# First attention of a four-layer kernel: row transposes in another order, q weights in two loads, mask copies later, one v product earlier

## The chip, the cores and the metric

The kernel runs on one core of one Trainium2 chip. Times are device microseconds (us) of one execution. A kernel is described by the median of its runs, with the lowest and the highest. Engines are named as the profile does: PE is TensorE, PEld its weight loads, DVE VectorE, ACT ScalarE, POOL GpSimd, SP SyncE, which here only issues DMAs. A "q" behind an engine's name marks a DMA issue in its queue.

## The reference

Four layers on x of 2048 x 576, each with a residual: attention A, mixer B, A, B. Only A matters here.

```python
def A(x, wqkv, wo):                      # x: layernormed, 2048 x 576, 32 heads of 18
    q, k, v = split(x @ wqkv)
    idx  = pos[:, None] - 2 * arange(8)  # each query sees 8 keys, every second one back
    attn = softmax(where(idx >= 0, q . k[idx] * 18**-0.5, -1e9))
    return (attn @ v[idx]) @ wo
x = x + A(layernorm(x), A_wqkv, A_wo)
x = x + B(layernorm(x), ...)             # gelu, 2048 x 2048 spatial mix, product
# ... and the same two again
```

## The kernel before

An attention tile is 112 queries; there are 19, each in two half steps, so the main loop runs over steps s = 0 to 37: scores (L_mm) for the next step, exponential (EXP), product with v (PV). Other work is hung on steps by `at(step, function, ...)`: projections PG of q and k, products VW for v, output projection WO, and behind it the layernorm of the next layer's input, LN_XN, with its row transpose LN_T, a DMA issued by SyncE. PG writes q and k into a staging buffer; DMAs then move them into QK, heads spread over the partitions. QK has extra rows for the window's mask, filled by VectorE (`fill_window_rows`).

```python
def fill_window_rows(self, QK, half):
    ...
    for g0 in (0, 4):                    # four copies of 128 x 4096
        for a in range(2):
            nc.vector.tensor_copy(out=QK[:, a, g0:g0 + 4, c0:c0 + n]..., in_=self.pat[...]...)

def load_wqk(self, eng):
    for c0, n, w0 in ((D, 512, D + 64), (0, D, 0), (D + 512, 64, D)):   # k, q, rest of k
        ...
# ---- schedule of an attention layer (li == 0: the first)
for i in range(NS):                      # 16 row blocks of 128
    ...
    at(s, WO, i, 0)                      # needs the row transpose oT<-o_t of its tile
    at(s + 1, WO, i, 1)
    at(s + 2, LN_XN, i)
    if i < NS - 1:
        at(max(s + 4, 24 + (5 * i) // 4) if li == 0 else s + 4, LN_T, i)
if li == 0:
    at(0, self.load_wo, nc.sync)         # 648 KB, needed from step 8
    for f in reversed(self.load_win2a(nc.gpsimd)):
        at(0, f)                         # 6 x 288 KB, needed in the mixer only
...
for k_, (d, qk, cc) in enumerate(pre):   # last projections ahead of the loop
    ...
    PG(d, qk, cc, li > 0 or k_ < 4, q2)
    if li == 0 and k_ == 3:
        self.fill_window_rows(QK, 1)
if li == 0:
    VW(nvw - 1, 0, False)
    VW(nvw - 1, 1, False)
for s in range(NST):
    if s + 1 < NST: L_mm(s + 1); EXP(s + 1)
    PV(s)                                # one more row transpose, oT<-o_t, for SyncE
    for f, a in table.pop(s, []): f(*a)
```

The softmax here doesn't subtract the row's maximum and nothing guards it: scores larger than these inputs give would overflow.

## Time and profile before

| | before |
|---|---|
| first three runs, median (lowest to highest) | 1191.1 us (1190.1 to 1191.19) |
| profiled run: span, granted clock | 1190.8 us, 0.998 |
| TensorE busy | 1180.2 us, 99% |
| first attention | 2 to 134 us |
| all 55 later runs beside the experiments | median 1191.9 us (1189.2 to 1195.4) |

The prediction below shows this kernel's profile line by line. TensorE is busy almost all the time, so a change in DMAs or other engines can win only idle TensorE time, or time in which its clock is halved.

One line that the prediction did not look at is SyncE's queue just before the loop (columns: start, length, engine and line, operation, destination<-source, count):

```profile
41.93 5.20 SPq L249 DMA_TRANSPOSE xnT<-ln_xn  x4
```

The fourth of these is issued by 47.14 us and lands, by its semaphore in the trace, at 50.02 us. The step-1 projection that reads it starts at 50.90 us. There is slack of 0.9 us, and nobody waits in this profile; so the line is easy to pass over.

### The profile page before, as it was taken

To read this page: it belongs to the slowest core of one execution; us is meant where nothing else is said; L and a number is where in the kernel's file an instruction comes from. 1 tells how busy PE (TensorE), PEld (TensorE's weight loads), DVE (VectorE), ACT (ScalarE), POOL (GpSimd) and SP (SyncE) were. 2 spreads that over 40 slices of the span, in tenths; PEclk is the share of its full clock that TensorE was granted. 3 is DMA by queue.
4 is the path that set the end of the run, shared out by engine and by line. 5 is a ranking of instruction groups with operands and counts; after the bars stand their busy time and mean duration, and the time that the engine had idled before them with its cause. 6 is when DMAs were issued, how large, how long until landed. Compare 5 with 4: busy or idle time off the path is not lost.

```text
span 1190.8 us, 20761 instructions
## 1 busy us (share of the span) xinstructions
PE 1180.2 (99%) x8554; PEld 620.6 (52%) x8554; DVE 547.4 (46%) x1206; ACT 376.6 (32%) x593; POOL 281.5 (24%) x383
## 2 busy tenths in 40 slices
PE   8999999999999999999999999999999999999998
PEld 5567544444444444457755775444444444444677
DVE  8688587333233233245556786753233233233311
ACT  5578677210110110202156786760110110111000
POOL 4768685000000000001153877530000000000000
PEclk9999999999999999999999999999999999999999
DMA  8989992000000000049645999900000000000332
GB/s 195 200 163 199 181 224 65 23 4 9 12 12 12 12 1 11 12 139 291 169 98 117 203 227 196 202 14 9 12 12 1 12 12 12 12 1 28 125 105 73
DMA packets 178104, 101.21 MB, mean 85 GB/s; under 512 B 134336, under 2 KB 159360, under 8 KB 178009
## 3 DMA queue, kind: packets, MB, share of 16 engines
q1 hardware_dynamic: 165144, 78.13, 30.6%
q0 software_dynamic: 6512, 16.00, 5.4%
q10 hardware_dynamic: 6352, 5.75, 1.6%
q8 instruction: 67, 1.10, 0.4%
q14 instruction: 29, 0.23, 0.1%
HBM read 42.39 MB, written 16.53 MB: 49 GB/s over the span
## 4 chain that ended last, share of the span: by engine, by line
PE 94%; DMA 3%; POOL 1%; ACT 0%; issue 0%; SPq 0%; DVE 0%; ACTq 0%; DVEq 0%
PE pg L887 42%; PE pz L869 12%; PE po L941 12%; PE pz L791 11%; PE pp L402 5%; PE pw L494 3%; PE O_ps L457 3%; PE pv L379 3%; PE L_ps L437 2%; DMA oT<-o_t 2%; PE pzs L791 1%; DMA QK<-win2a 1%; POOL QK L77 1%; DMA wqk_sb<-in_A_wqkv_dram 1%; ACT P_sb L446 0%
## 5 line engine op out<-in xcount | busy, mean ns | idle before, releaser
L887 PE MATMUL pg<-Wq,Z 128*128 128x512 bf16 x2304 | 502.8, 379 | 0.0
L887 PEld LDWEIGHTS <-Z 128*128 128x128 bf16 x2304 | 225.3, 98 | 272.0
L891 DVE TENSOR_TENSOR g_tmp<-pg,ln_xn 128x512 f32<-128x512 f32 x144 | 99.6, 692 | 429.2 <-PE pg L887 429.2
L881 ACT ACTIVATE z1T<-pz 128x1024 bf16<-128x1024 f32 x72 | 73.7, 1024 | 513.8 <-PE pz L869 513.6
L77 POOL DMA_DIRECT2D wout<-in_B_w_out_dram x4 | 4.3, 1064 | 604.6 <-PE pg L887 604.6
L941 PE MATMUL po<-wout,Z 128*128 128x288 bf16 x1152 | 141.4, 286 | 0.0
L446 ACT ACTIVATE P_sb<-L_ps 128x896 bf16<-128x896 f32 (+1 forms) x152 | 126.7, 887 | 41.2 <-PE L_ps L437 40.6
L869 PE MATMUL pz<-xnT,w 128*128 128x512 bf16 (+1 forms) x640 | 136.0, 380 | 0.0
L941 PEld LDWEIGHTS <-Z 128*128 128x128 bf16 x1152 | 112.7, 98 | 28.8
L791 PEld LDWEIGHTS <-xnT 128*128 128x128 bf16 (+1 forms) x800 | 66.2, 97 | 81.0 <-issue 23.7
L791 PE MATMUL pz<-win2a,xnT 128*128 128x512 bf16 x384 | 104.8, 380 | 0.0
L892 DVE TENSOR_TENSOR Z<-g_tmp,z1T 128x512 bf16<-128x512 f32 x144 | 99.6, 692 | 9.7
L869 PEld LDWEIGHTS <-w 128*128 128x128 bf16 (+1 forms) x640 | 51.1, 97 | 80.0 <-issue 27.1
L402 PE MATMUL pp<-xnT,wqk_sb 128*128 128x512 bf16 x360 | 83.8, 382 | 0.5 <-DMA wqk_sb<-in_A_wqkv_dram 0.5
L805 ACT ACTIVATE zp<-pz 128x1024 bf16<-128x1024 f32 x64 | 65.5, 1024 | 36.6 <-PE pz L791 32.8
L951 DVE TENSOR_TENSOR x_new<-po,xo 128x288 f32<-128x288 f32 (+1 forms) x64 | 28.8, 455 | 87.6 <-PE po L941 83.5
L791 PE MATMUL pz<-win2b,xnT 128*128 128x512 bf16 (+1 forms) x256 | 65.7, 380 | 0.0
L807 DVE CUSTOM_DVE_ANT_0 Z<-zp 128x1536 bf16<-128x1536 bf16 x32 | 56.6, 1769 | 13.1 <-ACT zp L805 13.0
L77 POOL DMA_DIRECT2D QK<-stg x81 | 50.7, 631 | 36.3 <-DVE stg L371 21.0
L379 PE MATMUL pv<-wv_sb,xnT 128*128 128x288 bf16 (+1 forms) x380 | 55.8, 285 | 0.0
L242 POOL TENSOR_SCALAR ln_xn<-x_new,ln_mv,ln_rstd 128x576 bf16<-128x576 f32 x23 | 52.8, 2294 | 2.0
L402 PEld LDWEIGHTS <-wqk_sb 128*128 128x128 bf16 x360 | 33.2, 98 | 37.2 <-DMA wqk_sb<-in_A_wqkv_dram 1.0
(114 smaller groups left out, 916.9 us busy)
## 6 DMA issues: line engine op xcount, KB each, us to landing
xres<-x_new SPq DMA_DIRECT2D x48, 288.0 KB
xo<-xres SPq DMA_DIRECT2D x32, 288.0 KB
wout<-in_B_w_out_dram POOLq DMA_DIRECT2D x4, 1296.0 KB, 8.5
xo<-xres SPq DMA_DIRECT2D x8, 576.0 KB
w<-in_B_w_in_dram SPq DMA_DIRECT2D x16, 256.0 KB
QK<-stg POOLq DMA_DIRECT2D x53, 72.0 KB, 4.4
QK<-stg SPq DMA_DIRECT2D x41, 72.0 KB
xo<-in_A_x_dram SPq DMA_DIRECT2D x8, 288.0 KB
```

The source lines that it names most:

```text
L77: return eng.dma_start(out=out, in_=in_)
L379: nc.tensor.matmul(pv[:nk, 0:288], lhsT=self.xnT[:, c, QT * t:QT * t + nk], rhs=wv_sb[:, c, hh * 288:(hh + 1) * 288], start=(c == 0), stop ...
L402: nc.tensor.matmul(pp[:, :], lhsT=w, rhs=self.xnT[:, c, PADL + cc * 512:PADL + (cc + 1) * 512], start=(c == 0), stop=(c == 4))
L446: nc.scalar.activation(out=P_bufs[(2 * s + jp) % 4][:nk, :, :, 0:nq], in_=Lv[:nk, :, :, 0:nq], func=ACT.Exp, scale=scale)
L791: nc.tensor.matmul(pzvs[ci][:, sub * 512:sub * 512 + w], lhsT=self.xnT[r0:r1, c, PADL + i * P:PADL + (i + 1) * P], rhs=win2(c)[r0:r1, c0 + ...
L805: nc.scalar.activation(out=zp[:, c0:c0 + cn], in_=pzvs[ci][:, 0:cn], func=ACT.Gelu_apprx_tanh, accum_out=sums[:, ci:ci + 1])
L869: nc.tensor.matmul(pz1s[q // 2][:, q % 2, :], lhsT=w1[r0:r1, c, sub * P:(sub + 1) * P], rhs=self.xnT[r0:r1, c, PADL + q * 512:PADL + (q + ...
L881: nc.scalar.activation(out=z1T[:, q2 * 512:(q2 + 2) * 512], in_=pz1s[q2 // 2][:, :, :].rearrange("p a b -> p (a b)"), func=ACT.Gelu_apprx_ ...
L887: nc.tensor.matmul(pg[:, :], lhsT=Z[:, jj, i, sub * P:(sub + 1) * P], rhs=Wq[q][:, i, :], start=(i == 0), stop=(i == NS - 1))
L891: nc.vector.tensor_tensor(out=tmp[:], in0=pg[:, :], in1=bsp[:, qs], op=ALU.add)
L892: nc.vector.tensor_tensor(out=uT(jj)[:, sub, qs], in0=tmp[:], in1=z1Ts[jj, sub][:, qs], op=ALU.mult)
L941: nc.tensor.matmul(acc[hh], lhsT=uT(j // 2)[:, j % 2, i * P:(i + 1) * P], rhs=wouts[j // NJH][:, j % NJH, hh * 288:(hh + 1) * 288], start= ...
```

## The change

The intent: let the first q product start on part of its weights; fill the stop before the first scores with a v product and take the mask copies out of GpSimd's way there; and spread the row transposes so that those of the attention output no longer queue behind them at the end.

```diff
-    def fill_window_rows(self, QK, half):
+    def fill_window_rows(self, QK, half, parts=((0, 0), (0, 1), (4, 0), (4, 1))):
...
-    def load_wqk(self, eng):
+    def load_wqk(self, eng, names=("k", "q", "k1")):
+        parts = dict(k=(D, 512, D + 64), q=(0, D, 0), q0=(0, 256, 0), q1=(256, D - 256, 256), k1=(D + 512, 64, D))
...
-                xn = stgs[(2 + k_) % NSTG]...
+                xn = stgs[(1 + k_) % NSTG]...
...
-            self.load_wqk(nc.sync)
+            self.load_wqk(nc.sync, ("k", "q0", "q1", "k1"))
...
-                VW(t, hh, li == 0)                 # last argument: evict on VectorE
+                VW(t, hh, li == 0 and t > 5)
...
-                    at(13 * hh, VW, t, hh, True)
+                    if hh == 1:
+                        at(0, VW, t, hh, True)
...
-                at(max(s + 4, 24 + (5 * i) // 4) if li == 0 else s + 4, LN_T, i)
+                at(s + 4 if li > 0 or i > 12 else 19 + 2 * i if i < 8 else 35 + (i - 8) // 2, LN_T, i)
         if li == 0:
+            at(1, self.fill_window_rows, QK, 1, ((4, 0),))
+            at(2, self.fill_window_rows, QK, 1, ((4, 1),))
             at(0, self.load_wo, nc.sync)
-            for f in reversed(self.load_win2a(nc.gpsimd)):
-                at(0, f)
+            w2l = self.load_win2a(nc.gpsimd)
+            for k_ in (3, 5, 4, 2, 1, 0):
+                at(0, w2l[k_])
...
-            if li == 0 and k_ == 3:
-                self.fill_window_rows(QK, 1)
...
             VW(nvw - 1, 1, False)
+            VW(nvw, 0, True)
+            self.fill_window_rows(QK, 1, ((0, 0), (0, 1)))
```

More of the change, by code (lines that the diff above doesn't have):

```diff
@@ L193, in fill_window_rows @@
         c0 = PADL + half * n
-        for g0 in (0, 4):
-            for a in range(2):
-                nc.vector.tensor_copy(out=QK[:, a, g0:g0 + 4, c0:c0 + n].rearrange("p g (k x) -> p g k x", x=256),
-                                      in_=self.pat[:, a, None, None, PADL:PADL + 256].to_broadcast([P, 4, n // 256, 256]))
+        for g0, a in parts:
+            nc.vector.tensor_copy(out=QK[:, a, g0:g0 + 4, c0:c0 + n].rearrange("p g (k x) -> p g k x", x=256),
+                                  in_=self.pat[:, a, None, None, PADL:PADL + 256].to_broadcast([P, 4, n // 256, 256]))
     def H_tile(self, name):
@@ L284, in zero_right @@
         nc.vector.memset(R["wo"][64:128, 4, :], 0.0)
-    def load_wqk(self, eng):
+    def load_wqk(self, eng, names=("k", "q", "k1")):
         R = self.right
-        for c0, n, w0 in ((D, 512, D + 64), (0, D, 0), (D + 512, 64, D)):
+        parts = dict(k=(D, 512, D + 64), q=(0, D, 0), q0=(0, 256, 0), q1=(256, D - 256, 256), k1=(D + 512, 64, D))
+        for c0, n, w0 in (parts[k_] for k_ in names):
             self.dma(R["wqk"][:, :, w0:w0 + n], self.A_wqkv[0:512, c0:c0 + n].rearrange("(c p) n -> p c n", p=P), eng=eng)
@@ L509, in LN_XN @@
                 k_, m = divmod(i - 4, 3)
-                xn = stgs[(2 + k_) % NSTG][:].rearrange("p a b -> p (a b)")[:, 640 * m:640 * (m + 1)]
+                xn = stgs[(1 + k_) % NSTG][:].rearrange("p a b -> p (a b)")[:, 640 * m:640 * (m + 1)]
             tails[i]["xn"] = self.ln_xn(tails[i]["x"], P, mv, rstd, nmr, eng="pool", xn=xn)
```

## The prediction

> **What bounds the kernel now.** I read the page first, then the busy times by stretch, then the engines in order of time around the few gaps, then the chain of waits. The page says that TensorE is the bound of the whole program:
>
> ```profile
> span 1190.8 us, 20761 instructions
> ...
> PE 1180.2 (99%) x8554; PEld 620.6 (52%) x8554; DVE 547.4 (46%) x1206; ACT 376.6 (32%) x593; POOL 281.5 (24%) x383
> ```
>
> All that is not TensorE is 1190.8 - 1180.2 = 10.6 us. The change touches the first attention only (about 2 to 134 us); the mixers and the second attention issue the same instructions in the same order. So nearly all of it is settled by idle and slow TensorE time in those 134 us. By stretch (columns: length; PE, PEld, DVE, ACT, POOL busy with counts; granted clock; DMA share; GB/s):
>
> ```profile
> 14.00:24.00 10.00, 9.53 (x49) 4.79 (x50) 8.70 (x29) 5.45 (x10) 1.71 (x2) 1.00 0.79 146
> ...
> 44.00:50.00 6.00, 5.24 (x57) 3.12 (x55) 5.60 (x7) 3.75 (x6) 5.43 (x7) 1.00 1.09 204
> 50.00:54.00 4.00, 4.00 (x68) 1.95 (x67) 2.14 (x5) 1.98 (x4) 1.05 (x2) 0.57 1.07 364
> ...
> 80.00:92.00 12.00, 11.47 (x237) 8.36 (x234) 10.33 (x33) 10.50 (x13) 11.23 (x14) 1.00 0.83 186
> 92.00:102.00 10.00, 9.57 (x198) 7.17 (x197) 7.25 (x23) 9.37 (x14) 9.50 (x10) 1.00 1.11 205
> ...
> 120.00:134.00 14.00, 12.18 (x208) 8.16 (x206) 10.65 (x33) 6.79 (x14) 10.21 (x11) 1.00 1.05 187
> ```
>
> TensorE lacks 0.47 us near 14 us, 0.76 at 44 to 50, 0.53 and 0.43 between 80 and 102, and 1.82 in the last 14 us; and from 50 to 54 us it is busy but at a granted clock of 0.57. That is the whole pool, about 5.3 us when the clock dip counts for 1.2. TensorE in order of time names the releasers:
>
> ```profile
> 14.47 1.90 PE L402 MATMUL pp<-xnT,wqk_sb 128*128 128x512 bf16 x8 [0.55 <-DMA wqk_sb<-in_A_wqkv_dram]
> ...
> 48.86 0.22 PE L437 MATMUL L_ps<-QK 32*128 32x112 bf16 x1 [0.69 <-DMA QK<-win2a]
> ...
> 50.90 2.29 PE L402 MATMUL pp<-xnT,wqk_sb 128*128 128x512 bf16 x5
> ...
> 125.22 0.79 PE L494 MATMUL pw<-wo_sb,oT 128*128 128x288 bf16 x5 [0.59 <-DMA oT<-o_t]
> ...
> 131.51 1.39 PE L494 MATMUL pw<-wo_sb,oT 128*128 128x288 bf16 x10 [1.23 <-DMA oT<-o_t]
> ```
>
> The group at 50.90 took 2.29 us; the same five matmuls take 1.24 us at 54.08 and later. The late waits are on the row transposes of the attention output. SyncE's queue shows why they are late:
>
> ```profile
> 121.02 1.78 SPq L469 DMA_TRANSPOSE oT<-o_t  x1
> 122.90 1.23 SPq L249 DMA_TRANSPOSE xnT<-stg  x1
> 124.18 0.57 SPq L77 DMA_DIRECT2D xres<-x_new  x1
> 124.84 1.23 SPq L249 DMA_TRANSPOSE xnT<-stg  x1
> 126.17 0.53 SPq L77 DMA_DIRECT2D xo<-in_A_x_dram  x1
> 126.80 1.19 SPq L469 DMA_TRANSPOSE oT<-o_t  x1
> ```
>
> Its source was complete at 123.0 (VectorE, o_t at 122.58 for 0.46), but the transpose was issued at 126.80, because two row transposes for the next layer's input stand before it; the chain of waits gives it 4.57 us from there to landing.
>
> **What the Trainium skill says.** (1) "TensorE: Matmul & The Clock Gate", "Part 1: The HAM clock gate": the clock falls to half for a free-running activity window of 3413 ns after a window without enough activity. The trace agrees on size and length: by half microseconds it is 0.52 at 50.5 and 0.57 at 53.5, about 3.4 us. It does not show a wholly idle window before it: from 47 to 50.5 only 0.69 us were idle, the rest being mostly short matmuls (K of 32, or 19 columns). (2) "SBUF — State Buffer", "SBUF: two separate sides": a VectorE operation in a two-port mode keeps GpSimd from writing the descriptors of its DMAs. The trace agrees:
>
> ```profile
> 44.65 1.34 POOL L77 DMA_DIRECT2D QK<-win2a  x1 [0.57 <-DMA QK<-win2a]
> 45.99 5.07 POOL L77 DMA_DIRECT2D win2a<-in_B_w_in_dram  x6
> ...
> 44.68 4.64 DVE L196 COPY QK<-win_pat 128x4096 bf16<-128x4096 bf16 x4
> ```
>
> The issue under the four mask copies took 1.34 us, the median of such issues is 0.59. (3) "DMA: Bandwidth & Descriptors", "Issuing engines are not separate DMA queues": all queues share 16 engines. The attention-output transpose issued at 90.38 landed after 9.51 us, while the DMA share of 92 to 102 us was 1.11.
>
> **The change part by part.** Comparing instruction order by engine: TensorE runs the same instructions; one group of five v matmuls leaves step 13, and one more stands ahead of the scores that wait at 48.86. VectorE gives four v evictions to ScalarE. SyncE has two more loads.
>
> Split q weights: the first q product waits 0.55 us for 648 KB; now the first 256 of 576 columns are a load of their own, 44% of the bytes. At the 306 GB/s of 7 to 17 us that is about 1.2 us earlier, so the 0.55 us go. But the next stop is the DMA chain to 48.8 us, which starts at GpSimd (27.34 to 38.26 us without a gap, held first by the mask copies until 28.9), and does not move with TensorE. So this gain alone would be waited away.
>
> Early v product, late mask copies: the scores that wait until 48.86 start at 47.28; they need 0.35 to 0.6 us, so about 1.3 us are lost there, not only the 0.69. The v group of 0.63 us fills half. The copies now stand behind that group's eviction (about 48 us), so GpSimd's last move at 44.65 is issued in about 0.6 instead of 1.34 us; and as the weight piece which must wait for that staging buffer is now first in GpSimd's queue, 2 x 288 KB no longer compete with it. I take the landing at 48.0. TensorE then is held by ScalarE instead: two exponentials of 0.92 us after these scores, the next scores need their PSUM buffers, 0.3 to 0.45 us. At step 13 the move leaves TensorE with 1.6 us of work against 1.84 us of ScalarE (2 x 0.92), so about 0.3 of the 0.63 us come back as a wait. Net of all early parts: 1.3 - 0.45 - 0.3 = 0.5 us.
>
> Clock dip: the window before it would now hold two v groups more closely packed and no idle. 1.05 us in the projection (2.29 - 1.24) plus 0.15 in the scores after it (0.51 against 0.35) = 1.2; with a chance of 85% to go: 1.0 us.
>
> VectorE's two copies after 48 us are 2 x 1.16, those at steps 1 and 2 one each. A step asks 0.72 + 0.69 = 1.4 us of VectorE in 2.1 us, so the delay of about 1.2 us is gone within some four steps; the four PSUM buffers cover it. I count 0.
>
> Row transposes: every odd step from 19 to 33 gets one, directly behind the tile's own transpose; where eight stood between steps 24 and 32 there are now five from 25 to 33, and those of row blocks 8 and on go behind step 35, after the last attention-output transpose. One transpose is 1.23 us of SyncE, so the last one is issued about 2.5 to 3.7 us sooner (not before 123.1) and lands at about 127.5, before TensorE wants it at 130.3. Both waits, 0.59 + 1.23 = 1.82 us, can go; I take 1.6. In exchange three row transposes enter 91 to 99 us, where DMA is fullest and a late transpose (the 9.51 us one) already stops VectorE for 1.59 us and TensorE for about 0.7. I charge 0.3.
>
> Sum: 0.5 + 1.0 + 1.6 - 0.3 = 2.8 us, that is 1191.1 - 2.8 = **1188.3 us**.
>
> **The rivals.** (a) The transposes only move the wait: those at steps 19 to 23 delay the attention-output transposes there, and the three o_t buffers stop VectorE. For it: share 1.11 and the 1.59 us wait at 99.99. Against it: SyncE stands free from 98.0 to 101.5. It would take back 1 to 2 us: 1189.5 to 1190. (b) ScalarE becomes the bound of steps 13 to 17, and whatever was gained at 48 us is waited for there. For it: exponentials without a gap for 3.35 us at 80.94 and again at 84.61. TensorE comes 1.7 us earlier, but ScalarE follows TensorE step by step before that, so it comes earlier too. If all were lost: 1189.8. (c) The clock dip is not removed, as the window runs free of the program, or falls at another place: 1189.5. (d) VectorE's late copies stall PSUM buffers in steps 0 to 4: 0.5 to 1 us lost. (e) Everything goes right: 1191.1 - 5 = 1186.
>
> **Range and chances.** The three runs of before span 1.1 us. The full pool gives 1186 as floor; (a) with (c) gives 1190.6. So 1186.3 to 1190.6. 2% are 24 us; no part is within reach of that: 0.98 within 2%, 0.01 each side.
>
> **What would show it.** Right: no DMA wait of about 0.55 near 14 us; GpSimd's last QK<-win2a issue near 0.6 us; no L_ps wait on QK<-win2a; clock 1.00 from 50 to 54 us; no pw wait on oT after 120 us; mixer matmuls starting some 2.8 us sooner. Wrong: idle TensorE on P_sb near step 0 or 13 over 0.8 us, new waits on oT between 90 and 110 us, or a half-clock window anywhere else in the span.

## More of the kernel before

The projection at step 1 reads columns 1536 to 2047 of the transposed input xnT. These come from four row transposes xnT<-ln_xn that SyncE issues at about 41 to 47 us.

## The result, and the profile after

| | before | after |
|---|---|---|
| median of six runs (lowest to highest) | 1191.68 us (1190.1 to 1193.0) | 1192.55 us (1192.02 to 1193.61) |
| ratio, 95% interval | | 1.0009 (0.9996 to 1.0022) |
| profiled run: span, clock | 1190.8 us, 0.998 | 1190.3 us, 0.998 |

A ratio is the mean time of one kernel's runs over that of the other's of the same rounds, so it is not quite the ratio of the medians quoted beside it. The 2.8 us did not come, and the median lies above the range.

The page of the changed kernel, first its span and TensorE's busy time:

```profile
span 1190.3 us, 20666 instructions
...
PE 1173.2 (99%) x8457; PEld 620.5 (52%) x8554; DVE 546.7 (46%) x1202; ACT 378.1 (32%) x597; POOL 278.1 (23%) x383
```

The 7 us less of PE are 97 matmul records missing from the trace, not less work: the 8554 weight loads are all there. (A group of matmuls marked x4 below, where x5 are issued, lacks such a record.) I therefore compare the kernels by the start of weight loads along the sequence. By stretch (same columns as in the prediction):

```profile
14.00:24.00 10.00, 9.95 (x52) 4.98 (x51) 9.05 (x32) 5.59 (x11) 1.71 (x2) 1.00 0.98 160
44.00:50.00 6.00, 5.28 (x59) 3.30 (x57) 2.76 (x5) 3.78 (x6) 2.98 (x5) 1.00 1.08 221
50.00:54.00 4.00, 3.95 (x75) 2.27 (x74) 3.50 (x8) 3.23 (x5) 1.19 (x3) 1.00 1.08 366
80.00:92.00 12.00, 10.34 (x209) 7.26 (x209) 8.50 (x28) 8.52 (x11) 11.13 (x13) 0.86 1.03 166
92.00:102.00 10.00, 9.72 (x201) 7.21 (x199) 7.51 (x23) 9.41 (x14) 9.11 (x9) 1.00 1.14 266
120.00:134.00 14.00, 13.85 (x221) 9.66 (x221) 12.04 (x37) 8.47 (x15) 11.28 (x12) 1.00 0.95 182
```

Against the same stretches of before: the gap at 14 us is gone (9.53 to 9.95), the clock is 1.00 at 50 to 54 us instead of 0.57, and the last stretch rose from 12.18 to 13.85. But 80 to 92 us fell from 11.47 to 10.34 with a clock of 0.86: the half-clock window is not gone, it stands elsewhere. TensorE in order of time:

```profile
48.44 0.22 PE L437 MATMUL L_ps<-QK 32*128 32x112 bf16 x1 [0.48 <-DMA QK<-win2a]
48.83 0.22 PE L437 MATMUL L_ps<-QK 32*128 32x112 bf16 x1 [0.17 <-DMA QK<-win2a]
...
50.85 1.24 PE L402 MATMUL pp<-xnT,wqk_sb 128*128 128x512 bf16 x4
...
85.59 0.79 PE L494 MATMUL pw<-wo_sb,oT 128*128 128x288 bf16 x5 [1.40 <-DMA oT<-o_t]
```

The scores still wait until 48.8 us. The projection takes 1.24 us instead of 2.29. At 85.59 us there is a wait of 1.40 us that before did not have: the row transpose of tile 5 was issued at 78.89 and landed at 85.54 us (before: 79.01 and 83.34). The half-clock window of 3.41 us follows at 86.43 us. GpSimd's queue at the loop's start and SyncE's at its end:

```profile
44.77 0.51 POOL L77 DMA_DIRECT2D QK<-win2a  x1 [0.88 <-DMA QK<-win2a]
45.29 1.68 POOL L77 DMA_DIRECT2D win2a<-in_B_w_in_dram  x3
49.20 1.98 POOL L77 DMA_DIRECT2D win2a<-in_B_w_in_dram  x3 [2.23 <-DMA QK<-win2a]
```

```profile
121.72 0.89 SPq L77 DMA_DIRECT2D xres<-x_new  x1
122.69 0.38 SPq L77 DMA_DIRECT2D xo<-in_A_x_dram  x1
123.80 1.20 SPq L469 DMA_TRANSPOSE oT<-o_t  x1
```

The last QK move is issued in 0.51 us instead of 1.34, as predicted, and lands at 48.78 instead of 48.81. And the first three weight pieces, which took 1.15 us each in before, now take 0.56 each and are all issued by 46.97 us (before 49.44). The last attention-output transpose is issued at 123.80 instead of 126.80 and lands at 126.96 us: no wait on oT is left after 120 us.

The lead of TensorE over before's profiled run (negative is ahead), with the later profiles that the argument needs. The first column compares the same instruction, the first product with v, which starts at 49.01 us in before; the others compare the same number of weight loads. (By number the first column would flatter the kernels with the early v product by up to 1.3 us: they have loaded five weights more by then. At 58 us the two ways differ by 0.2 us at most.)

| at before's time of | 49.01 us | 58 us | 97 us | 123 us | 134 us | last matmul |
|---|---|---|---|---|---|---|
| after | -0.03 | -1.16 | +0.97 | +0.69 | -1.08 | -0.95 |
| e9, the same kernel again | -1.21 | +1.77 | +1.91 | +1.63 | -0.14 | +0.01 |
| e13, in effect the same kernel | -1.47 | -1.04 | -0.90 | -1.18 | -2.95 | -2.05 |
| e1, new row order alone | -0.01 | +0.05 | +0.05 | -0.18 | -2.23 | -2.21 |

From 123 to 134 us every profile with the new row order gains 1.7 to 2.2 us. From the first product with v to 97 us the changed kernel loses 1.0, 3.1 and 0.6 us. The experiments look for the cause of that.

### The profile page after: what moved, and what is told of

Read it like the earlier page. It is cut to its first block, busy times and chain, and to the rows that moved or that the text cites. A ratio compares the mean times of both kernels' runs of the same rounds, so it can differ in the third digit from the quotient of the medians. Undisturbed runs are those within 1.5% of the kernel's fastest.

```text
span 1190.3 us, 20666 instructions
## 1 busy us (share of the span) xinstructions
PE 1173.2 (99%) x8457; PEld 620.5 (52%) x8554; DVE 546.7 (46%) x1202; ACT 378.1 (32%) x597; POOL 278.1 (23%) x383
## 4 chain that ended last, share of the span: by engine, by line
PE 95%; DMA 1%; POOL 1%; issue 1%; DVE 1%; ACT 1%; POOLq 0%
PE pg L891 42%; PE pz L873 12%; PE po L945 12%; PE pz L795 11%; PE pp L402 5%; PE pw L494 3%; PE pv L379 3%; PE O_ps L457 3%; PE L_ps L437 2%; PE pzs L795 1%; DMA QK<-win2a 1%; POOL QK L77 1%; DMA oT<-o_t 1%; ACT P_sb L446 0%; DVE ln_st L554 0%
## 5 line engine op out<-in xcount | busy, mean ns | idle before, releaser
L402 PE MATMUL pp<-xnT,wqk_sb 128*128 128x512 bf16 x341 | 81.2, 379 | 0.9
```

The source lines that it names most:

```text
L402: nc.tensor.matmul(pp[:, :], lhsT=w, rhs=self.xnT[:, c, PADL + cc * 512:PADL + (cc + 1) * 512], start=(c == 0), stop=(c == 4))
```

## The experiments

Eighteen kernels ran, in five batches of three or four; the kernels of a batch shared a chip and 11 runs of before. All gave correct results. Expectations were written before each batch, so the early ones speak of the theory of that time: that the new wait on oT at step 16 (85.59 us) and the half-clock window behind it had taken the gain.

### e1: the row transposes alone

```diff
 # before, plus
+ xn = stgs[(1 + k_) % NSTG]...
+ at(s + 4 if li > 0 or i > 12 else 19 + 2 * i if i < 8 else 35 + (i - 8) // 2, LN_T, i)
```

> Kernel before plus the moved row transposes (and the staging buffers they write to) alone. Theory (pacing): the two waits of the output projection after 120 us (0.59 and 1.23 us) go, the half-clock window near 50 us stays, and as TensorE is not ahead at step 16 there is no new wait at 84 to 86 us; 1.0 to 1.8 us faster than before. Rival (the moved row transposes cause the new wait of 1.40 us): a wait on oT or o_t of 1 us or more between 84 and 110 us, time equal to before or slower.

Measured: 1190.77 us (1188.94 to 1193.46), ratio 0.9996 (0.9982 to 1.0009), before 1191.94. Its stretches:

```profile
50.00:54.00 4.00, 3.78 (x66) 1.92 (x66) 1.92 (x5) 1.91 (x4) 0.72 (x2) 0.57 1.08 371
120.00:134.00 14.00, 13.95 (x221) 9.39 (x221) 12.12 (x38) 7.76 (x14) 11.42 (x13) 1.00 0.81 169
```

The clock dip of before is there (0.57), the late waits are gone (13.95 of 14.00 busy). The middle costs nothing: +0.05 us at 97 us. So this part does what it should, 2.2 us in the profile; in the times, whose interval includes 1, the gain is not clear of noise.

### e2: everything but the row transposes

```diff
 # the changed kernel, minus
- xn = stgs[(1 + k_) % NSTG]...            (back to 2 + k_)
- at(... 19 + 2 * i if i < 8 ..., LN_T, i) (back to the old order)
```

> The changed kernel with the row transposes where the kernel before had them; all early parts kept. Theory (pacing): TensorE comes 1.0 to 1.5 us ahead to step 16 and waits there for the attention-output transpose of tile 5, 1 us or more, though no row transpose was moved; both late waits (1.8 us together) are back; within 1 us of before, 1 to 1.8 us slower than the changed kernel. Rival (row transposes cause the wait): no wait at 84 to 86 us, TensorE 1 us ahead of before at 110 us.

Measured: 1193.22 us (1192.68 to 1194.72), ratio 1.0018 (1.0005 to 1.0031). Its TensorE:

```profile
52.56 1.24 PE L402 MATMUL pp<-xnT,wqk_sb 128*128 128x512 bf16 x4 [1.66 <-DVE o_t L464]
...
131.22 1.39 PE L494 MATMUL pw<-wo_sb,oT 128*128 128x288 bf16 x10 [1.43 <-DMA oT<-o_t]
```

The late wait is back, as it should be. The wait at step 16, which the theory wanted, is not there; but TensorE is not ahead by then either. New is the wait of 1.66 us before the step-1 projection. The profile puts it to VectorE's o_t, which ended at 52.33 us, 0.23 us before the start. The last xnT<-ln_xn transpose landed at 52.47 us, 0.09 us before it. This run hardly tells the two apart; e4 does. Without the new row order the early parts are not a gain but a loss.

### e3: extra work after the stop

```diff
 # the changed kernel, plus
+ def extra():                             # five unread matmuls of 512 columns
+     ...
+ at(5, extra)
```

> The changed kernel plus five matmuls of 512 columns (about 1.09 us of TensorE) at step 5 that nobody reads. Theory (pacing): the time up to step 16 is not TensorE's, so the wait there shrinks from 1.40 to about 0.3 us, step 17 starts at 86.8 as before, and the whole is not over 0.3 us slower; if the wait also set off the half-clock window, that window goes and the kernel is up to 1 us faster. Rival (TensorE's own time sets it, the wait moves along): 1.1 us slower and a wait of 1.4 us.

Measured: 1194.1 us (1192.51 to 1194.77), ratio 1.002 (1.0008 to 1.0032). Its profile has no wait on oT at step 16: the transpose of tile 5 landed 2.08 us after its issue, against 5.39 in the first profile. The ratio to before rose by 0.0011 over the changed kernel's 1.0009, some 1.3 us, about the 1.24 us that five such matmuls take. That fits a kernel in which no wait at step 16 hides the extra work; but each of the two ratios is uncertain by 0.0012 or more to each side, so it is not shown.

### e4: more of the q and k moves on GpSimd

```diff
- at(1 + k_ if li == 0 else ..., PG, d, qk, cc, True)
+ at(1 + k_ if li == 0 else ..., PG, d, qk, cc, True, *((q2,) if li == 0 else ()))
```

> The changed kernel with two thirds instead of half of the q and k moves of steps 1 to 12 issued from GpSimd, so fewer from SyncE. If SyncE's queue in order is what makes the transpose of tile 5 late (issued 78.9 us, its source complete near 74): issued about 2 us sooner, landed before 84.2, no wait at step 16, 1.4 to 2.5 us faster than the changed kernel. If the shared DMA engines are: issued sooner but landed after 85 all the same, the wait stays over 1 us, time as the changed kernel.

Measured: 1192.49 us (1189.72 to 1195.43), ratio 1.0008 (0.9994 to 1.0023). No wait at step 16 in its profile, but 2.34 us before the step-1 projection, put to o_t again. But there o_t had ended at 51.68 us, and the last input transpose landed at 52.49 us, 0.10 us before the start at 52.59: it is the transpose. The theory of step 16 no longer explained the time: the wait is gone and the time stays. It went because TensorE came late, 1.60 us behind before at 58 us; the transpose of tile 5, issued 1.00 us sooner than in the first profile, landed only 0.31 us sooner. (e13 is the clearer case: ahead, and no wait at step 16.)

### A new theory

Of the first four experiments' profiles, e2, e3 and e4, those with the early parts, all had TensorE waiting at step 1 for xnT. Theory 1: the early parts bring TensorE to step 1 sooner and at the same time make that transpose land later, as the win2a loads are now issued sooner. Rival 2: VectorE is late with its copies. Rival 3: the landing has nothing to do with those loads.

### e5 and e6: both weight loads at step 3

```diff
- at(0, self.load_wo, nc.sync)
+ at(3, self.load_wo, nc.sync)
- at(0, w2l[k_])
+ at(3, w2l[k_])
```

e5 is the changed kernel with this edit, e6 is e1 with it.

> The changed kernel with the loads of wo and of the six win2a pieces issued three steps later (step 3 instead of step 0, some 6 us). Theory 1 (the early part is paced by the last row transpose xnT<-ln_xn, which shares the DMA engines with these loads): that transpose lands by 49.5 us, no pp wait before the step-1 projection, TensorE 1 us or more ahead of the kernel before at 54 us; the time is below that of the changed kernel by up to 1 us unless the wait at step 16 takes it again. Rival 2 (VectorE's late mask copies hold the step-1 projection): landing earlier, but the pp wait of 1.2 us or more stays. Rival 3 (the landing does not depend on the weight loads): it lands at 50 to 52.5 us as before.

> The kernel before with the new order of row transposes alone, and the weight loads at step 3. Theory 1: the last xnT<-ln_xn transpose lands by 49.5 us, TensorE at most 0.5 us better than in the run with the rows alone (its next stop, the QK<-win2a move at 48.8 us, is not moved, or moves by less than 0.8 us); median 1189.8 to 1190.8. If the weight loads at step 3 now collide with the row transposes of the attention output: a wait on oT before step 10 and a median above 1191.5.

Measured: 1201.41 us (ratio 1.0074) and 1203.64 us (1.0093). The early part went as theory 1 says: the transpose landed at 49.30 and 48.23 us, 1.59 and 1.42 us after its issue, no wait at step 1, TensorE ahead by 1.36 and 2.25 us at 58 us. Theory 1 was wrong about e6, which it allowed 0.5 us only: the QK move landed sooner too (47.36 us). Then wo came too late:

```profile
74.65 1.12 PE L494 MATMUL pw<-wo_sb,oT 128*128 128x288 bf16 x4 [8.11 <-DMA wo_sb<-in_A_wo_dram]
```

Issued at 61 us among the q and k moves, the two loads of wo took 13.3 and 15.2 us to land. At step 0 they took 3.3 to 9.6 in the other profiles.

### e7: the mask copies back at their place

```diff
 # the changed kernel, with
+ if li == 0 and k_ == 3: self.fill_window_rows(QK, 1)
- self.fill_window_rows(QK, 1, ((0, 0), (0, 1)))     and those at steps 1 and 2
```

> The changed kernel with all four mask copies back at their place behind the fourth projection; the v group stays early. Rival 2 (late copies hold VectorE): the pp wait at step 1 goes and the time falls by 0.5 to 1.5 us against the changed kernel. Theory 1: the copies do not matter for step 1, whose start stays within 0.2 us of the landing of the last xnT<-ln_xn transpose; GpSimd's last QK<-win2a issue is 1.3 us long again and the scores wait until 48.8 us or later; time within 0.7 us of the changed kernel.

Measured: 1191.45 us (1189.43 to 1193.66), ratio 0.9993 (0.9977 to 1.0009); two of six runs at 1189.4. The transpose landed at 49.84 us, no wait at step 1, 2.82 us ahead at the end. This looks like rival 2. But in e3, e4, e9 and e12 the operation of VectorE that is named had ended 0.2 to 0.8 us before the transpose landed, and in e5, with late copies and an early landing, step 1 did not wait. The copies act on the landing, in a way that I don't fully see: in e7 the first three weight pieces were issued as fast (0.56 us each, by 45.23 us) as in the changed kernel, and the last three were slowed, as in e9 and e13.

### e8: the rows and the split q load

```diff
 # e1, plus
+ self.load_wqk(nc.sync, ("k", "q0", "q1", "k1"))
```

> The kernel before with the new order of row transposes and the split q load, without the early v group and the late copies. Theory 1: TensorE 0.6 us ahead up to 47 us, all of it given back at the QK<-win2a wait (48.8 us), so 0.0 to 0.2 us against the run with the rows alone: 1190.2 to 1191.2 if that run is 1190.8. If the early v group and the late copies cost 1 to 1.5 us, this one is faster than the changed kernel by that much; if they cost nothing, the two are within 0.5 us.

Measured: 1193.95 us (1189.2 to 1197.37), ratio 1.001 (0.9988 to 1.0032). In the profile the 0.66 us gained at 25 us are +0.06 at 49 us: waited away, as predicted. The median misses; the spread goes with the clock: 1189.2 us with a mean granted clock of 1.000, 1197.37 with 0.996. TensorE, though not ahead, was stopped twice at row transposes of the attention output:

```profile
86.10 0.79 PE L495 MATMUL pw<-wo_sb,oT 128*128 128x288 bf16 x5 [0.77 <-DVE ln_rstd L221]
...
91.14 0.79 PE L495 MATMUL pw<-wo_sb,oT 128*128 128x288 bf16 x5 [0.59 <-DMA oT<-o_t]
```

(The first wait is put down to VectorE, but the transpose landed at 86.05 us, 0.05 us before the start, as in the wait of 1.40 us above: 85.54 and 85.59.) The profiles of before and e2, the two with the old row order, have no wait on oT between 58 and 120 us.

### e9: the changed kernel again

No edit.

> The changed kernel itself, unaltered, beside the next three on the same chip. Theory 1 (no fixed wait took the gain, but where the DMA landings and the half-clock windows happen to fall in a run): the wait of 1.40 us at step 16 and the half-clock window at 86 us are not there again in this profile, or smaller; instead the pp wait at step 1 behind the last xnT<-ln_xn transpose is; runs spread over 3 us, with the clock. Rival (a fixed structure): the same wait of over 1 us at step 16. Median 1192 to 1193 either way.

Measured: 1192.92 us (1192.21 to 1194.32), ratio 1.0007 (0.9994 to 1.002). No wait at step 16 this time. TensorE and GpSimd at step 1:

```profile
49.67 0.56 PE L457 MATMUL O_ps<-v_ext,P_sb 128*128 128x19 bf16 x16
51.61 2.29 PE L402 MATMUL pp<-xnT,wqk_sb 128*128 128x512 bf16 x5 [1.38 <-DVE rec L463]
53.84 0.58 PE L437 MATMUL L_ps<-QK 32*128 32x112 bf16 x16
54.35 0.60 PE L457 MATMUL O_ps<-v_ext,P_sb 128*128 128x19 bf16 x16
54.80 2.29 PE L402 MATMUL pp<-xnT,wqk_sb 128*128 128x512 bf16 x5
```

```profile
44.02 1.68 POOL L77 DMA_DIRECT2D win2a<-in_B_w_in_dram  x3
```

TensorE is 1.21 us ahead at the first product with v. It waits 1.38 us at step 1, and from 50.57 us the clock is halved for 6.83 us, two windows: the projections take 2.29 us twice. At 58 us it is 1.77 us behind. The last 11 us of the attention bring this to -0.14. This is the zero that the times show.

### e10, e11: win2a spread over steps 2 to 12

```diff
- at(0, f)                    # e10: e1 with this
+ at(2 + 2 * k_, f)           # e11: the changed kernel with the same
```

> The kernel before with the new order of row transposes, and the six win2a pieces at steps 2, 4, ... 12 instead of all at step 0; wo stays at step 0. Theory 1 (early part paced by DMA landings): last xnT<-ln_xn transpose by 49.0 us, wo landed by 53 us, no wait on wo_sb at step 8; TensorE 0.5 to 2 us ahead of the kernel before at 60 us, 2.5 to 4 ahead at 134 us; median 1188.5 to 1190.0. Rival (the competition of win2a does not matter, wo or the moves do): nothing ahead at 60 us, median as the rows alone, 1190.8.

> The changed kernel with the six win2a pieces at steps 2, 4, ... 12. Theory 1: the last xnT<-ln_xn transpose lands by 49.5 us, no pp wait at step 1, TensorE 1 to 2 us ahead of the kernel before at 60 us; median 1189 to 1191, that is 1.5 to 3 us below the changed kernel. Rival (late mask copies or the early v group cost the time): no better than the changed kernel by over 0.7 us.

Measured: e10 1189.67 us, ratio 0.9982 (0.9969 to 0.9994); e11 1192.43 us, 1.0006 (0.9994 to 1.0019). Both mended the landing (47.50 and 49.26 us), neither waits at step 1. e10 was 2.61 us ahead up to 84 us but 0.38 at 97: a group of scores at 85.25 us took 1.37 us instead of 0.56, waiting in part for QK<-stg moves, and a half-clock window followed at 86.72 us. e11 met a wait of 1.06 us on oT at 72.84 us, whose transpose took 7.1 us. Theory 1's time for e11 is missed.

### e12: output projection of row block 4 a step later

```diff
+ s += li == 0 and i == 4
```

> The changed kernel with the output projection of row block 4 and what follows it one step later. If the wait at step 16 is what costs the time in most runs: it goes, and the median falls by 1 to 1.5 us against the changed kernel of the same rounds. Theory 1 (it was one draw among several): no oT wait at step 16, but the median within 0.6 us of the changed kernel.

Measured: 1195.8 us (1191.17 to 1197.37), ratio 1.0021 (1.0004 to 1.0039). No wait at step 16, and slower; both expected times are missed. In its profile step 1 waits 1.80 us, with two half-clock windows, and two more follow at 88.06 us; three of its six runs have a clock of 0.994. Why this edit draws so many windows stays open.

### e13: win2a behind step 1

```diff
- at(0, w2l[k_])
+ at(1, w2l[k_])
```

> The changed kernel with the six win2a pieces behind step 1 instead of step 0, nothing else. Theory 1 (these loads overtake the last xnT<-ln_xn transpose): it lands by 50.0 us, at most 2.5 us after its issue; no pp wait at step 1 and no half-clock window of 6.8 us; TensorE at 58 us at least 1 us ahead of the kernel before; median 1190 to 1191.5. Rival (something else in the early part costs the time): the landing is earlier, the median still 1192 or more.

Measured: 1192.18 us (1189.32 to 1194.28), ratio 1.0 (0.9981 to 1.002). The edit did nothing: GpSimd has no instruction between the two places, so it ran ahead and issued the first three pieces by 45.85 us as ever. The transpose landed at 51.19 us, 5.20 after its issue, and step 1 waited 1.04 us (here VectorE ended at 51.18 us, so this run does not tell the two apart). It serves as a third look at the changed kernel, one in which no half-clock window fell into the attention: 2.95 us ahead at 134 us, the 2.8 us of the prediction.

### e14, e15: what keeps e11 from e10

e15 is e10 with the split q load; e14 is e11 with all mask copies at their old place:

```diff
 # e15: e10, plus
+ self.load_wqk(nc.sync, ("k", "q0", "q1", "k1"))
 # e14: e7, plus
- at(0, w2l[k_])
+ at(2 + 2 * k_, w2l[(3, 5, 4, 2, 1, 0)[k_]])
```

> The changed kernel with all four mask copies at their old place and the six win2a pieces at steps 2 to 12. If the late mask copies are what keeps e11 from e10: 1189 to 1190. If the early v group or the v evictions on ScalarE keep it: 1191.5 to 1192.5 as e11, with waits on P_sb or oT between 70 and 95 us.

> The kernel before with the new order of row transposes, the split q load and the six win2a pieces at steps 2 to 12. The q split alone is waited away at the QK<-win2a move, so as e10: 1189 to 1190.3; last xnT<-ln_xn transpose by 49 us. If the q split itself costs something: 1191 or more.

Measured: e14 1193.18 us, ratio 1.0015 (0.9995 to 1.0034); e15 1192.04 us, 1.0005 (0.9987 to 1.0023). Both early parts are as theory 1 has them: landing at 48.29 and 48.52 us, no wait at step 1, 2.19 and 1.85 us ahead at 58 us. The times of both are missed. e14's TensorE meets this:

```profile
87.34 1.38 PE L494 MATMUL pw<-wo_sb,oT 128*128 128x288 bf16 x5 [3.37 <-DMA oT<-o_t]
```

with two half-clock windows from 84.47 us; 3.16 us behind at 97 us. So not the late copies alone kept e11 back. A TensorE that comes early is often stopped later: between 58 and 97 us the lead shrank by 1.4 to 5.4 us in the first profile and in e10, e11, e14 and e15, but by 0.1 to 0.7 us only in e7, e13 and e17.

### e16, e17, e18: the rest of the question

```diff
 # e16: e10 with the edit of e4; e17: e10 unaltered
 # e18: the changed kernel with
- at(0, w2l[k_])
+ at(3, w2l[k_])
```

> e10 with the moves of the in-loop projections two thirds on GpSimd, one third on SyncE (before: half and half). If the place in SyncE's queue delays the oT transposes at 65 to 92 us: they are issued 0.5 us or more sooner, no oT or P_sb wait over 0.5 us between 70 and 95 us, the lead of 2 us or more at 60 us is kept at 100 us, median 0.5 to 1.5 us below e17. If the 16 DMA engines are what is short: issued sooner, landing at the same time, lead lost as in e10, median within 0.5 us of e17.

> e10 unaltered: last xnT<-ln_xn transpose by 49.0 us, TensorE 1.5 to 2.6 us ahead of the kernel before at 60 us; median 1189.5 to 1190.8, ratio 0.998 to 0.999. If e10 was a fortunate draw: 1191 to 1192, as e15.

> The changed kernel with all six win2a pieces behind step 3, so behind the moves of the projections of steps 1 to 3 (issue at 57 us or later); wo stays. Theory 1: last xnT<-ln_xn transpose at most 2.5 us after its issue and by 49.5 us, no pp wait at step 1; TensorE at 58 us 1 to 2.5 us ahead of the kernel before. Then six loads meet the oT transposes of 60 to 80 us, so I expect oT waits at steps 8 to 12 of 0.5 to 2 us; median 1191 to 1193. If the landing is over 50.5 us, it is not these loads.

Measured: e16 1198.89 us, ratio 1.0062; e17 1191.03 us (1189.07 to 1193.47), 0.9992 (0.9974 to 1.0011); e18 1198.36 us, 1.0052.

e16: the oT transposes were issued sooner, as meant (62.07 us against 63.25 in e17), and landed later: 9.06 us after their issue against 4.21. So a sooner issue did not help: this speaks for the second reading, that the DMA engines are short, though the time, 7.9 us above e17 instead of within 0.5, was not foreseen. e17: the advantage of e10 shrank to within the noise. e18:

```profile
50.60 1.24 PE L402 MATMUL pp<-xnT,wqk_sb 128*128 128x512 bf16 x5
...
76.93 1.38 PE L494 MATMUL pw<-wo_sb,oT 128*128 128x288 bf16 x5 [3.87 <-DMA oT<-o_t]
```

```profile
58.05 2.24 POOL L77 DMA_DIRECT2D win2a<-in_B_w_in_dram  x4
```

This is the run that e13 should have been. With only win2a later, the transpose lands at 49.14 us, 2.38 us after its issue, and step 1 does not wait. But the same loads now meet the oT transposes: the one issued by 65.58 us landed at 76.89. The cost was expected in kind and is larger than expected (1191 to 1193 us).

### What the runs show together

The last xnT<-ln_xn transpose, from the end of its issue to its landing, in all twenty profiles:

| kernels | latency | wait at step 1 |
|---|---|---|
| win2a at the loop's start, copies late: after, e2, e3, e4, e9, e12, e13 | 3.9 to 5.3 us | 1.0 to 2.3 us, in six of seven |
| win2a at the loop's start, copies early: before, e1, e7, e8 | 2.9 to 3.4 us | none |
| win2a at step 2 or later: e5, e6, e10, e11, e14 to e18 | 1.4 to 2.4 us | none |

The groups do not overlap. In all six profiles with a wait the projection starts 0.09 to 0.10 us after this landing. That the win2a loads delay the transpose is shown by e18 against the changed kernel, and again by the pairs that differ in these loads alone: e1 and e10, e7 and e14, e8 and e15. How the mask copies act on it is not settled.

The second part is the clock. In the 55 runs of before, 22 had a mean granted clock of 1.000 (mean 1190.55 us), 21 had 0.999 (1192.39), 12 had 0.998 or less (means 1193.4 to 1195.1 by value). One window of 3.41 us at half clock is, worked out, 1.7 us of lost matmul time, or 0.0014 of the mean clock. In the 17 runs of the changed kernel (six first ones, e9, e13) only 4 had 1.000, and 10 had 0.998 or less. But the clock is not all: the 4 runs at 1.000 have a mean of 1190.84 us, no better than before's 1190.55. In the profiles a window mostly begins within a few us of a wait or of the sparse first scores.

A third part lies outside the first attention. e10, e13 and e17 lost another 0.9 to 1.5 us of their lead in the second attention, where before has no such wait:

```profile
691.79 0.79 PE L494 MATMUL pw<-wo_sb,oT 128*128 128x288 bf16 x5 [1.35 <-DMA oT<-o_t]
```

This is e10's; e7 and e15 kept all their 2.8 us, and why is open.

## Why the prediction was wrong

- **Split q weights**: right. The wait near 14 us is gone, the gain was waited away by 49 us (e8: +0.06).
- **The landing at 48.0 us**: its working ("2 x 288 KB no longer compete with it") failed in part. The issue took 0.51 us as said; but the piece that had to wait was the fourth in the queue (2.23 us), not the first, and three pieces were issued right behind the move, by 46.97 us. Nor does the length of the issue set the landing: in e1 it took 0.55 us, and the move landed at 48.81 us as in before. The landing was 48.78 in the first profile, 47.3 to 47.6 in e9, e12 and e13, and in e10 and e17, one kernel, 46.13 and 47.89.
- **"Net of all early parts: ... 0.5 us"**: this is the step that failed. It ended at the first scores. The next stop was 2 us further on, a landing at 50.02 us with 0.9 us of slack, which I never listed. In seven profiles with all early parts this landing came at 50.16 to 52.49 us, and in six of them TensorE waited 1.0 to 2.3 us for it. The same loads that I credited with leaving the QK move alone hold it back: without them it came at 49.14 us (e18). That it is their sooner issue which makes it later than in before is not shown: in e7 they were issued as soon, and it landed at 49.84. In the seven profiles the first product with v came 0.03 to 1.60 us sooner than in before, but by 58 us five were 0.2 to 2.0 us behind it; two were 1.0 to 1.2 ahead.
- **Clock dip, "with a chance of 85% to go: 1.0 us"**: wrong. It was gone from 50 to 54 us in the first profile and fell at 86 us; in e9 it was doubled. This is rival (c), to which I gave too little.
- **ScalarE, "0.3 to 0.45 us" behind the first scores**: right in size, 0.25 to 0.40 in e3, e4, e12 and e13.
- **Step 13, "about 0.3 ... come back"**: all of the 0.63 us came back; the step takes 2.22 us either way, with a new wait of 0.43 us on P_sb. So rival (b) is there, in small.
- **VectorE's copies, "I count 0"**: right for VectorE itself; rival (d) is not seen as such.
- **Row transposes, "I take 1.6"**: right. 1.7 to 2.2 us from 123 to 134 us in all profiles with the new order, 0.4 in e2 without it.
- **"I charge 0.3" for 91 to 99 us, and rival (a)**: no cost there in e1. But the first profile waited 1.40 us on oT at step 16, and e8, which is not ahead, 0.77 and 0.59 us at 86 and 91 us; the two profiles with the old row order have no such wait. So rival (a) is not excluded: several profiles with the new order have no such wait either, and how often it comes was not measured.
- **The range**: built on three runs that span 1.1 us. Before alone spans 6.2 us over 55 runs, and one half-clock window is worth 1.7 us. The rivals' sizes were not added up in full either: (a) at its 2 us and (c) at 1.2 would make 1191.5, not 1190.6 (and the pool adds up to 5.2, not 5.3). The run with no window in the attention, e13's profile, was 2.95 us ahead at 134 us and 2.05 at the end; the mean is not ahead.
- **The signs**: of the good ones, four came in the first profile (at 14 us, the issue of 0.51 us, the clock at 50 us, no late wait on oT). The wait for the QK move did not go (0.48 and 0.17 us), the mixer came 1.08 us sooner and not 2.8, and of the bad ones the half-clock window came, at 86 us.

What stays open: how the mask copies change the landing in e7; why windows of half clock come more often in the changed kernel, since waits alone do not fix where they fall; and whether the new row order itself makes the oT waits near 86 us. No version is shown to beat both kernels: e10 did at 0.9982, its repetition e17 at 0.9992 does not stand clear of 1.

## What to carry to other kernels

When a change lets an engine arrive sooner, list every landing in the next few microseconds with its slack, not only the one that is waited for today; and ask which loads will be issued sooner with it. Weights that are needed much later can push back a small transfer that is needed now, but moved into a full stretch they cost more. Before sizing a gain of 3 us, take more than three runs, sort them by granted clock, and check in the trace that an edit of the program moved the issue in time.

## What the Trainium skill lacked or had wrong

- "TensorE: Matmul & The Clock Gate", "Part 1: The HAM clock gate": the window of 3413 ns and the half clock agree (3.41 us or multiples, 0.5). Its table has the cold state follow an idle window; only of another kernel, with short idle times between groups of matmuls, does it tell that the clock fell back without one, and it gives no size for that. Here half-clock windows came with no idle window before them, such as before's at 50.52 us with 0.76 us idle from 47 to 50.5. It calls warm-up variable from run to run; the runs show that for a whole kernel: 1.8 us between the means of runs at 1.000 and 0.999.
- "DMA: Bandwidth & Descriptors", "Queues, rings and completion order": it says that each DMA engine goes round the queues that have work, packet by packet; no run here tests that by itself. It has no figure for what other loads do to one small DMA transpose: from the end of its issue to its landing the last xnT<-ln_xn took 1.4 us in e14 and 5.3 in e12, and an oT<-o_t beside six weight loads and the q and k moves 11.3 us (e18).
- "SBUF — State Buffer", "SBUF: two separate sides": GpSimd's issues under VectorE's copies took 1.15 to 1.34 us in before, without them 0.51 to 0.59 in the changed kernel, which agrees; in e1 one issue took 0.55 us where one copy gave way to the next, at 45 us. No page says whether a load that is freed in this way delays another transfer; here the win2a loads held back a transpose (e18).
- No page warns that a wait for several semaphores may be put down to the wrong one: in e4 the profile names VectorE's o_t, done at 51.68 us, where the start at 52.59 us followed a transpose that landed at 52.49 us.
